# Block-causal attention with a Fourier feed-forward on one core: the row maxima of two heads taken together, one exponential per piece, and PSUM banks in one pool

## The chip, the cores and the metric

The kernel runs on one core of one Trainium2 chip. The metric is the device time in microseconds; the time before is the median of three runs. The profile is that of one further execution. The five engines are named as in the profile: PE is TensorE (matmuls, with PEld for its weight loads), DVE is VectorE, ACT is ScalarE, POOL is GpSimd, SP is SyncE, which here issues most DMAs. PSUM, which PE writes, has eight banks of 128 partitions x 512 float32.

## The reference

```python
def _attn_ref(q, k, v):            # (8 batches, 8 heads, 576 positions, 64)
    scores = scale * q @ k^T       # scale = 1 / 8
    mask = block_i >= block_j      # blocks of 64 positions
    scores = np.where(mask, scores, -1e9)
    scores = scores - np.max(scores, axis=-1, keepdims=True)
    attn = np.exp(scores); attn = attn / (np.sum(attn, -1, keepdims=True) + 1e-09)
    return attn @ v

x = heads side by side             # (8, 576, 512)
X = np.fft.fft(np.fft.fft(x, axis=1), axis=2)
u = x + np.real(X)
un = (u - mean) / np.sqrt(var + 1e-6)          # over the last axis
out = u + np.maximum(un @ w_ch1, 0.0) @ w_ch2  # 512 -> 2048 -> 512
```

## The kernel before

Most of it is near-float32 precision made of smaller parts: in attention and feed-forward a value is split into a high and a low float16 part ("ph" and "pl" for the probabilities, "uh" and "ul", "gh" and "gl", "VH" and "VL"), and a product is three matmuls.

**Attention.** 64 heads go one after another, in pairs (g = h // 2) where they share a load. `load_pair` brings q and k of two heads to 128 partitions, 64 for each head. `sum_qk` and `scale` find a power of two, `high` and `low` write the two float16 parts into two pair tiles, `a` (high q, then low k) and `b` (low q, then high k). `high_copies` and `low_copies` are DMAs that lay each head out again for the matmuls, as a "lead" tile (64 rows of high parts, then 8 rows of masks and one row for the maxima) and a "rest" tile. From them `max_part` computes a head's scores of the high parts alone, in four parts of one PSUM bank each. Queries are taken in five tiles j of 128 rows that start 64 before a multiple of 128, so the block at the end of a tile's keys is allowed only for its upper 64 rows; the mask rows in "lead" add a large negative number there, which makes the matmul 72 rows deep. DVE reduces each bank to row maxima, "M". `shift` turns M by a small matmul ("ident, M", 5 columns), ACT scales it to "mt", and a DMA writes mt into the last row of "lead". Then `scores` makes the real scores in four pieces of up to 512 columns (two matmuls per chunk, rest and lead), ACT takes the exponential twice, once to float16 (ph) and once to float32 (p), and POOL makes pl = p - ph. `values` multiplies by V (the "av" matmuls) and divides by the sums.

**Fourier.** After the eight heads of a batch, `mirror` reads the rows back, `folded` adds and subtracts mirrored halves (cosine and sine folds, tiles "fs"), `stage1` and `stage2` are matmuls with tables of cosines and sines ("dft"), and the result is added to x in "u". Cosine folds and sine folds share the tiles fs0 and fs1, so for batches 1 to 7 the order is cosine folds, cosine stage 1, sine folds, sine stage 1.

**Feed-forward.** `normalized_steps` normalizes 256 rows and transposes them; they are a "feed", numbered me = 1 to 18. A feed's first half writes "h" tiles (two 128-column groups of hidden units in one bank), ACT and DVE take them out as gh and gl; the second half accumulates in "acc". The last three feeds use a form with seven products in place of eight.

**The order.** The build keeps a clock of its own and queues with assumed costs for each engine. Work is cut into steps; a `Step` has an emit function, PE cost, a chain of costs on other engines ("D0.65" is 0.65 us on DVE, "B" marks where its bank is free again), the steps it comes after, whether it needs a PSUM bank, and a place. Ten lanes (loads, pairs, copies, maxima, scores, values, transforms) each hold one next step. The loop takes the step with the lowest place among those that are ready by the assumed clock, and otherwise a step of the feed ("filler"). The order found is then fixed on every engine. The banks: 3 "ps" for attention and Fourier, 2 "h" and 2 "acc" for feeds, 1 "av"; until the first feed starts, attention may use all seven of the first three kinds (`lent`).

The parts of a head's maxima before (tile j, first key, last key):

```python
MAXPARTS = (((0, 0, 64), (4, 512, 576), (1, 0, 192)), ((2, 0, 320),), ((3, 0, 448),), ((4, 0, 512),))
```

Line 229 is the helper that issues every matmul, line 232 that of the transposes, line 203 the wrapper of every other engine's instruction, so the profile's groups are told apart by their tiles.

Of the kernel before, what the change touches and what calls it, by code (L numbers as in the profile page):

```python
# [51 lines left out]

SEVEN = range(15, 18)

# [97 lines left out]
class Step:  # L152
# [8 lines left out]
    bank: bool = False  # L161
# [48 lines left out]
def tile_attn_fourier_ffn(  # L210
# [7 lines left out]
    ps = {name: pool(name, n, space=PSUM) for name, n in BANKS.items() if name != "ps"}  # L218
    turned = [(pool(f"ps{i}", 1, space=PSUM), f"ps{i}") for i in range(BANKS["ps"])]
    dram = pool("dram", 3, space=DRAM)  # L220

    def ps_tile():
        if current == "ps":
            turned.append(turned.pop(0))
            return turned[-1][0].tile([P, 512], F32, name=turned[-1][1])
        return ps[current].tile([P, 512], F32, name=current)
# [39 lines left out]
    def half_tiles(i):  # L266

        if i not in halved:
            a = work.tile([P, (64 + 2 * S) // (1 if i < HF else 2)], F32, name=f"lead{i}", bufs=1).bitcast(F16)
            b = work.tile([P, 2 * S // (1 if i < HF else 2)], F32, name=f"rest{i}", bufs=1).bitcast(F16)  # L270
            halved[i] = (a[0:KS, 0:64 + 2 * S], b[:, 0:2 * S]) + ((a[:, 64 + 2 * S:64 + 4 * S], b[:, 2 * S:]) if i < HF else ())
# [6 lines left out]
    def split(g):  # L278

        if g == GF:  # L280
            return tuple(stage[i].rearrange("p c d -> p (c d)").bitcast(F16)[:, 0:2 * S] for i in range(2))
        return half_tiles(g % 2)[2:4]

    M = [const.tile([P, 6], F32R, name=f"M_{i}") for i in range(2)]
# [3 lines left out]
    ZT = const.tile([P, NCOS], F32R, name="ZT")  # L288
    for i in range(HF):
# [18 lines left out]
    current = "ps"  # L308
    rings = {name: [0.0] * n for name, n in BANKS.items()}
# [8 lines left out]
    def ready(step):  # L318
        r = max((done[x] for x in step.after), default=0.0)
        if step.bank:  # L320
            return max(r, min(rings[x][0] for x in lent))
# [27 lines left out]
    def issue(step):  # L349
        nonlocal current, now  # L350
# [7 lines left out]
        free = None  # L358
        starts = []
        for engine, cost in step.chain:  # L360
            if engine == "B":
                free = t + HOP
# [15 lines left out]
        if step.bank:  # L378
            current = min(lent, key=lambda x: rings[x][0])
            rings[current] = rings[current][1:] + [t if free is None else free]  # L380
# [48 lines left out]
    def high(g):  # L429
        (rq, rk), sc = raws["pair", g], scales[g]  # L430
        a, b = split(g)
        scalar.activation(a[:, 0:S], rq, AF.Copy, scale=sc[:, 1:2])
# [4 lines left out]
    def low(g):  # L437
        (rq, rk), sc = raws.pop(("pair", g)), scales[g]
        a, b = split(g)
        vector.scalar_tensor_tensor(b[:, 0:S], rq, sc[:, 1:2], a[:, 0:S], op0=ALU.mult, op1=ALU.subtract)  # L440
        yield
        vector.scalar_tensor_tensor(a[:, S:], rk, sc[:, 2:3], b[:, S:], op0=ALU.mult, op1=ALU.subtract)
        yield

    def high_copies(h):
# [5 lines left out]
        sync.dma_start(x[0:D, 64:64 + S], a[at, 0:S])  # L451
# [3 lines left out]
    def low_copies(h):  # L455
# [3 lines left out]
        sync.dma_start(x[D:P], a[at])  # L459
# [161 lines left out]
    def max_part(h, n):  # L621

        m = M[h % 2]
# [25 lines left out]

    def shift(h):  # L650

        t = ps_tile()
        mm(t[0:5, 0:P], M[h % 2][:, 0:5], ident_r, start=True, stop=True)
# [26 lines left out]
    def scores(h, n):  # L680
# [78 lines left out]
    def score_lane():  # L759
        for h in range(B * H):  # L760
            for n, (i, at, chunks) in enumerate(PIECES):
                w = sum(x[2] for x in chunks)
                yield Step(
                    lambda n=n: scores(h, n), w / 1200.0, (_a(w), "p1", _a(w), "B", _g(w), "p"),
# [4 lines left out]
    def max_lane():  # L769
        for h in range(B * H):  # L770
# [5 lines left out]
            yield Step(lambda: shift(h), 0.12, ("A0.26", "B", "Q0.6", "M0.05", "L1.6"), (("M", h),), ("X", h), True, place=h - 0.6)  # L776

# [13 lines left out]
    def fourier_steps(b):  # L791
# [23 lines left out]
        def folded(op, width, name, c):  # L815
# [128 lines left out]
        def folds(name, op, width):  # L944
            for c in (2, 0, 1):
                yield Step(
                    lambda c=c: folded(op, width, name, c), 0.0, ("t1",) + (("X1.6", "A1.2", "X0.9") if c == 2 else ("X1.12", "A0.41", "X0.43")) + ("t",), (D_("u"),) + ((("F", 1),) if b == 1 else ()),
# [631 lines left out]
```

## Time and profile before

| | us |
|---|---|
| median of 3 runs | 1211.73 (1210.74 to 1212.89) |
| the profiled execution | 1207.94 |
| its span, first to last instruction | 1206.1 |
| PE busy | 1138.9 (94%) |
| DVE busy | 742.1 (62%) |
| ACT busy | 604.5 (50%) |
| POOL busy | 482.5 (40%) |
| mean granted PE clock | 0.961 of full |

The page cuts the span into 40 slices of about 30 us and gives each engine's busy share in tenths. Matmuls overlap in PE's pipeline, so a matmul's duration is longer than what it keeps the next one waiting. A row of the timeline has the start, the duration, the engine, the line, what is written from what, rows x columns of the weights, the shape that streams, and the number of instructions merged into it; in square brackets, idle time before it and what ended it.

### The profile page before, as it was taken

The numbers are of one execution on the slowest core, as the hardware profiler recorded it, in microseconds if no ns is written. First come the engines' busy times: TensorE is split into PE (matmuls) and PEld (weight loads), VectorE is DVE, ScalarE is ACT, GpSimd is POOL, SyncE is SP. The second block draws the span as 40 slices with busy tenths as digits, with TensorE's granted clock in tenths as the row PEclk, the third lists the DMA queues.
The fourth block names the chain that finished last, engine by engine and source line by source line (L and its number), as shares of the span: only waits on it lengthen the run. The fifth ranks groups of instructions, "written<-read, shape, count | busy, mean of one in ns | idle before, by whom it ended". The sixth has DMA issues, their size and how long they took to land.

```text
span 1206.1 us, 26181 instructions
## 1 busy us (share of the span) xinstructions
PE 1138.9 (94%) x10338; PEld 840.6 (70%) x10338; DVE 742.1 (62%) x1615; ACT 604.5 (50%) x1338; POOL 482.5 (40%) x630
## 2 busy tenths in 40 slices
PE   5767788999899999999999999999999999999998
PEld 4544475676677777777777777777677767788885
DVE  6877886666847673666647475757475657454421
ACT  5656667755565555536555346545554323233320
POOL 4552624534434434243442424353334333545420
PEclk9758789999799999999999999999999999999999
DMA  8785453333323342323325133413240010000000
GB/s 260 224 246 170 144 132 99 95 111 89 109 57 118 95 115 67 86 66 104 90 67 158 34 85 112 128 31 104 69 124 16 29 40 19 23 10 10 18 18 18
DMA packets 66128, 108.27 MB, mean 90 GB/s; under 512 B 9671, under 2 KB 36209, under 8 KB 66006
## 3 DMA queue, kind: packets, MB, share of 16 engines
q1 hardware_dynamic: 58662, 82.25, 24.1%
q10 hardware_dynamic: 4384, 16.78, 4.2%
q0 software_dynamic: 2960, 7.58, 2.1%
q8 instruction: 81, 1.33, 0.5%
q14 instruction: 41, 0.34, 0.1%
HBM read 58.50 MB, written 18.89 MB: 64 GB/s over the span
## 4 chain that ended last, share of the span: by engine, by line
PE 83%; DVE 5%; DMA 4%; POOL 3%; ACT 3%; issue 1%; SPq 0%; ACTq 0%; DVEq 0%; POOLq 0%
PE h L229 30%; PE acc L229 28%; PE ps L229 16%; PE av L229 8%; DMA lead<-mt 2%; DVE W L203 1%; POOL u L203 1%; PE ps L232 1%; DVE M L203 1%; POOL pl L203 1%; ACT p L203 1%; ACT ph L203 1%; ACT W L203 1%; DVE VL L203 1%; DMA lead<-rest 1%
## 5 line engine op out<-in xcount | busy, mean ns | idle before, releaser
L229 PE MATMUL h<-uh,W 128*128 128x256 f16 x2304 | 432.2, 274 | 0.2 <-DVE gl L203 0.2
L203 POOL TENSOR_TENSOR pl<-p,ph 128x288 f16<-128x288 f32 (+1 forms) x256 | 259.4, 1024 | 365.3 <-ACT p L203 337.0
L229 PEld LDWEIGHTS <-W 128*128 128x128 f16 x3456 | 332.7, 98 | 60.4 <-issue 1.3
L229 PE MATMUL h<-ul,W 128*128 128x256 f16 x1152 | 315.3, 274 | 0.0
L229 PE MATMUL acc<-W,gh 128*128 128x512 f16 (+1 forms) x1008 | 289.5, 370 | 0.0
L203 DVE TENSOR_REDUCE M<-ps 128x1 fp32r<-128x320 f32 (+3 forms) x293 | 131.3, 484 | 119.3 <-PE ps L229 118.8
L229 PE MATMUL acc<-W,gl 128*128 128x512 f16 (+1 forms) x504 | 186.2, 370 | 0.0
L229 PE MATMUL ps<-lead 73*128 73x288 f16 (+8 forms) x708 | 161.4, 291 | 15.4 <-DMA lead<-in_c_masks_dram 6.8
L203 ACT ACTIVATE ph<-ps 128x288 f16<-128x288 f32 (+1 forms) x235 | 119.5, 510 | 111.4 <-PE ps L229 110.6
L203 ACT ACTIVATE gh<-h 128x512 f16<-128x512 f32 x138 | 82.5, 598 | 166.6 <-PE h L229 161.6
L203 DVE SCALAR_TENSOR_TENSOR gl<-h,gh 128x512 f16<-128x512 f32 x138 | 94.7, 687 | 114.9 <-ACT gh L203 114.3
L229 PEld LDWEIGHTS <-ph 128*128 128x128 f16 x2112 | 133.1, 103 | 26.8 <-issue 4.6
L229 PEld LDWEIGHTS <-gh 128*128 128x128 f16 x1056 | 98.4, 99 | 67.8 <-issue 4.7
L229 PE MATMUL av<-VH,pl 128*128 128x65 f16 (+1 forms) x963 | 117.0, 201 | 8.4 <-POOL pl L203 6.5
L203 ACT ACTIVATE p<-ps 128x288 f32<-128x288 f32 (+1 forms) x235 | 119.0, 508 | 2.2 <-POOL pl L203 1.0
L229 PE MATMUL av<-VH,ph 128*128 128x65 f16 (+1 forms) x966 | 118.4, 203 | 0.7 <-ACT p L203 0.7
L229 PE MATMUL av<-VL,ph 128*128 128x64 f16 x960 | 116.7, 200 | 0.0
L229 PEld LDWEIGHTS <-pl 128*128 128x128 f16 x1056 | 103.5, 102 | 12.7 <-POOL pl L203 8.5
L229 PE MATMUL ps<-rest 128*128 128x320 f16 (+3 forms) x356 | 99.4, 292 | 1.0 <-DVE M L203 0.9
L229 PEld LDWEIGHTS <-lead 73*128 73x128 f16 (+1 forms) x744 | 66.7, 103 | 36.4 <-issue 8.1
L229 PEld LDWEIGHTS <-gl 128*128 128x128 f16 x528 | 51.5, 98 | 55.3 <-issue 0.5
L229 PEld LDWEIGHTS <-rest 128*128 128x128 f16 x372 | 38.8, 104 | 34.9 <-issue 15.3
(255 smaller groups left out, 1611.1 us busy)
## 6 DMA issues: line engine op xcount, KB each, us to landing
raw<-in_qk_dram SPq DMA_DIRECT2D x30, 576.0 KB
W<-in_moe_w_ch_dram ACTq DMA_DIRECT2D x14, 1024.0 KB
V<-in_v_dram SPq DMA_DIRECT2D x32, 320.0 KB
rest<-lead SPq DMA_DIRECT2D x64, 144.0 KB
rest<-rest SPq DMA_DIRECT2D x60, 144.0 KB
out_dram<-u SPq DMA_DIRECT2D x32, 256.0 KB
xd<-x SPq DMA_DIRECT2D x30, 256.0 KB
lead<-lead SPq DMA_DIRECT2D x60, 72.0 KB
```

The lines of the kernel that those rows point to most:

```text
L203: x = f(*args, **kw)
L229: return tc.keep_in_program_order(nc.tensor.matmul(*args, **kw))
L232: return tc.keep_in_program_order(nc.tensor.transpose(*args, **kw))
```

## The change

- `pair_max` replaces `max_part` for pairs g >= 8, which are heads 16 to 63. It reads the pair tiles a and b directly, 64 rows for each head: head 0 of the pair on rows 0 to 63, head 1 on rows 64 to 127, each into a bank of its own, their matmuls issued in turn. The mask rows are gone: the five blocks that only the upper 64 rows may see are matmuls of their own and are reduced for partitions 64 to 127 alone (DIAG); the rest goes to MAIN, and M is the larger of both. A head then has 9 matmuls in place of 6, with the same 1600 columns.
- To serve as weights with queries from 64 before the start, tile a gets 64 zero columns ahead (`high`, `low`, `sum_qk` and the copies move by 64; a memset on POOL for the first three pairs).
- M has four buffers in place of two.
- From head 17 on, `scores` takes one exponential, to float32, and a copy on ACT makes the float16 part from it; the bank is free after the exponential.
- After feed 2 the "h" banks join "ps" in one pool of five. From then on an "h" tile takes the bank that is free first and holds it until gh and gl are made. A pair's maxima need two banks of one pool at once; while such a step has its inputs, steps that need one bank and have a higher place stand back.
- All batches now order the Fourier work as cosine folds, sine folds, cosine stage 1, sine stage 1; the sine folds of batches 1 to 7 take tiles from "un" (those of the normalized rows), and come after the transposes of the feed before.
- The first steps of `weight_parts` take their bank one yield earlier.

```diff
+ONCE = 17
+LEAST = -3.0e38
+GP = 8
...
-    M = [const.tile([P, 6], F32R, name=f"M_{i}") for i in range(2)]
+    M = [const.tile([P, 6], F32R, name=f"M_{i}") for i in range(4)]
+    MAIN, DIAG = ([const.tile([P, 5], F32, name=f"{x}_{i}") for i in range(2)] for x in ("MAIN", "DIAG"))
...
+    for i in range(2):
+        gpsimd.memset(MAIN[i], LEAST)
+        gpsimd.memset(MAIN[i][0:64, 0:1], 0.0)
+        gpsimd.memset(DIAG[i], LEAST)
     for i in range(HF):
         gpsimd.dma_start(LEAD[i][D:KS], c_masks)
...
     def sum_qk(g):
         (rq, rk), acc = raws["pair", g], sums(g)
         a, b = split(g)
-        scalar.activation(a[:, 0:S], rq, AF.Square, accum_out=acc[:, 1:2])
+        if g < GF + 3:
+            gpsimd.memset(a[:, 0:64], 0.0)
+        scalar.activation(a[:, 64:64 + S], rq, AF.Square, accum_out=acc[:, 1:2])
...
+    PAIRPARTS = (((0, 0, 64), (1, 128, 192), (2, 256, 320), (3, 384, 448), (4, 512, 576), (1, 0, 128)), ((2, 0, 256),), ((3, 0, 384),), ((4, 0, 512),))
+
+    def pair_max(g, n):
+
+        a, b = split(g)
+        ts = [ps_tile() for _ in range(2)]
+        at = 0
+        for i, (j, lo, hi) in enumerate(PAIRPARTS[n]):
+            for x, t in enumerate(ts):
+                rows_ = slice(D * x, D * (x + 1))
+                mm(
+                    t[:, at:at + hi - lo], a[rows_, P * j:P * (j + 1)], b[rows_, S + lo:S + hi], start=(i == 0),
+                    stop=(i == len(PAIRPARTS[n]) - 1), skip_group_check=True,
+                )
+            at += hi - lo
+        yield
+        for x, t in enumerate(ts):
+            main, diag = MAIN[x], DIAG[x]
+            if n == 0:
+                vector.tensor_reduce(
+                    diag[64:128], t[64:128, 0:320].rearrange("p (x y) -> p x y", y=64), axis=AX.X, op=ALU.max
+                )
+                vector.tensor_reduce(main[:, 1:2], t[:, 320:448], axis=AX.X, op=ALU.max)
+            else:
+                vector.tensor_reduce(main[:, n + 1:n + 2], t[:, 0:P * (n + 1)], axis=AX.X, op=ALU.max)
+            if n == 3:
+                vector.tensor_tensor(M[(2 * g + x) % 4][:, 0:5], main, diag, op=ALU.max)
+            yield
...
-        scalar.activation(ph[:, at:at + w], t[:, 0:w], AF.Exp, scale=0.125)
-        yield
+        if h < ONCE:
+            scalar.activation(ph[:, at:at + w], t[:, 0:w], AF.Exp, scale=0.125)
+            yield
         p32 = work.tile([P, 512], F32, name="p32", bufs=2)
         scalar.activation(p32[:, 0:w], t[:, 0:w], AF.Exp, scale=0.125)
         yield
+        if h >= ONCE:
+            scalar.copy(ph[:, at:at + w], p32[:, 0:w])
+            yield
         gpsimd.tensor_tensor(pl[:, at:at + w], p32[:, 0:w], ph[:, at:at + w], op=ALU.subtract)
...
+        for g in range(GP, B * H // 2):
+            for n in range(4):
+                d = f"D{(0.78, 0.42, 0.56, 0.91)[n]}"
+                yield Step(
+                    lambda n=n: pair_max(g, n), 0.06 + sum(x[2] - x[1] for x in PAIRPARTS[n]) / 2400.0, (d, "B", d),
+                    (("hi", g),), ("M", 2 * g) if n == 3 else None, 2, place=2 * g - 1.6,
+                )
...
-                if b == 0 and name == "s":
-                    t = work.tile([P, 2, 256], F32R, name="uh", bufs=2)
+                if name == "s":
+                    t = work.tile([P, 2, 256], F32R, name="un" if b else "uh", bufs=2)
...
-        order = (folds(*cos), folds(*sin), stages("c"), stages("s")) if b == 0 else (folds(*cos), stages("c"), folds(*sin), stages("s"))
+        order = (folds(*cos), folds(*sin), stages("c"), stages("s"))
...
-                gs[f] = ps["h"].tile([P, 512], F32, name="h")
+                gs[f] = ps_tile() if me > 2 else own_tile()
...
+        if not shared_out and ("F", 2) in done:
+            shared_out.append(True)
+            rings["ps"] += rings.pop("h")
...
+        claim = min((heads[i].place for i in able if heads[i].bank == 2 and max(done[x] for x in heads[i].after) <= now), default=None)
+        if claim is not None:
+            able = [i for i in able if heads[i].bank != 1 or heads[i].place <= claim]
```

More of the change, by code (lines that the diff above doesn't have):

```diff
@@ L160 @@
     key: object = None
-    bank: bool = False
+    bank: int = 0
+    hold: object = None
+    drop: object = None
     need: tuple = ()
@@ L217, in tile_attn_fourier_ffn, with next_banks, first @@
     ps_av = pool("ps_av", 1, space=PSUM)
-    ps = {name: pool(name, n, space=PSUM) for name, n in BANKS.items() if name != "ps"}
-    turned = [(pool(f"ps{i}", 1, space=PSUM), f"ps{i}") for i in range(BANKS["ps"])]
+    accs = pool("acc", BANKS["acc"], space=PSUM)
+    rings = {name: [[0.0, pool(f"{name}{i}", 1, space=PSUM), f"{name}{i}"] for i in range(BANKS[name])] for name in ("ps", "h")}
+    rings["acc"] = [[0.0, accs, "acc"] for _ in range(BANKS["acc"])]
+    given, held, shared_out = [], {}, []
     dram = pool("dram", 3, space=DRAM)
     def ps_tile():
[L223 to L226, printed above, removed]
+        _, pool_, name = given.pop(0)
+        return pool_.tile([P, 512], F32, name=name)
+    def next_banks(n):
+        def first(x):
+            return (sorted(rings[x], key=lambda y: y[0]) if shared_out else rings[x])[:n]
+        return min(((x, first(x)) for x in lent if len(rings[x]) >= n), key=lambda x: max(y[0] for y in x[1]))
     def mm(*args, **kw):
@@ L320, in ready @@
         if step.bank:
-            return max(r, min(rings[x][0] for x in lent))
+            return max(r, *(x[0] for x in next_banks(step.bank)[1]))
         if step.place > H and not step.cost:
@@ L357, in issue @@
                 x.forget(now)
-        free = None
+        free = []
         starts = []
@@ L378, in issue @@
         if step.bank:
-            current = min(lent, key=lambda x: rings[x][0])
-            rings[current] = rings[current][1:] + [t if free is None else free]
+            ring, got = next_banks(step.bank)
+            rings[ring] = [x for x in rings[ring] if not any(x is y for y in got)] + got
+            for n, x in enumerate(got):
+                x[0] = float("inf") if step.hold else free[min(n, len(free) - 1)] if free else t
+            if step.hold:
+                held[step.hold] = got[0]
+            given[:] = got
+        if step.drop in held:
+            held.pop(step.drop)[0] = t
         parts = step.emit()
@@ L769, in max_lane @@
     def max_lane():
-        for h in range(B * H):
+        for h in range(2 * GP):
             for n in range(4):
@@ L1073, in second @@
             if f == 0:
-                acc.append(ps["acc"].tile([P, DM], F32, name="acc"))
+                acc.append(accs.tile([P, DM], F32, name="acc"))
             gh, gl = gs[f]
@@ L1191, in both_steps @@
                     after = (("t", me, 0), ("t", me, 1)) + ((("g", me, k - 2),) if k > 1 else ())
-                yield Step(lambda part=part: both(k, part), 0.654, (), after, ("h", me, k) if last else None)
+                yield Step(
+                    lambda part=part: both(k, part), 0.654, (), after, ("h", me, k) if last else None, 0 if part else 1,
+                    hold=None if part else ("h", me, k),
+                )
         def split_steps(k):
@@ L1211, in feed_steps @@
             if not seventh:
-                seventh.append(turned.pop(0))
-                taken.append(rings["ps"].pop(0))
+                one = min(rings["ps"], key=lambda x: x[0])
+                rings["ps"] = [x for x in rings["ps"] if x is not one]
+                seventh.append(one[1:])
             nk = NF // 2
@@ L1525, in tile_attn_fourier_ffn @@
             if len(lent) > 1:
-                now = max(now, ready(filler), *rings["h"], *rings["acc"])
+                now = max(now, ready(filler), *(x[0] for x in rings["h"] + rings["acc"]))
                 lent = ["ps"]
```

49 lines of the change are left out of this document (28 added, 21 removed).

## The prediction

> **What bounds the kernel now.** I read the page's busy shares first, then its slices.
>
> ```profile
> PE 1138.9 (94%) x10338; PEld 840.6 (70%) x10338; DVE 742.1 (62%) x1615; ACT 604.5 (50%) x1338; POOL 482.5 (40%) x630
> PE   5767788999899999999999999999999999999998
> PEclk9758789999799999999999999999999999999999
> PE 83%; DVE 5%; DMA 4%; POOL 3%; ACT 3%; issue 1%; SPq 0%; ACTq 0%; DVEq 0%; POOLq 0%
> ```
>
> TensorE (PE) is the only engine near full and carries 83% of the chain that ended last. But the slices show three stages: up to about 240 us PE has holes and a low granted clock, one more dent follows near 300 us, and then it is solid. The table by stretches gives the sizes (columns: length, busy us and count of each engine, granted clock, DMA share, GB/s).
>
> ```profile
> core 0: us, PE busy (x) PEld busy (x) DVE busy (x) ACT busy (x) POOL busy (x), PEclk, DMA share, GB/s
> 240.00:290.00 50.00, 50.00 (x480) 36.26 (x478) 31.64 (x78) 26.65 (x63) 16.19 (x18) 1.00 0.28 81
> 290.00:304.00 14.00, 10.42 (x109) 7.82 (x107) 10.98 (x26) 8.10 (x20) 10.08 (x14) 1.00 0.59 167
> 304.00:318.00 14.00, 10.60 (x80) 7.29 (x80) 12.37 (x29) 7.83 (x20) 7.73 (x12) 0.52 0.54 151
> 330.00:1040.00 710.00, 710.00 (x6665) 517.40 (x6663) 431.78 (x976) 344.94 (x786) 273.17 (x330) 1.00 0.28 78
> ...
> L203 ACT ACTIVATE mt<-ps x48: 249/266/267, 242.0 to 934.8; 5x128 f16<-5x128 f32 x48
> ```
>
> From 330 to 1040 us PE is busy 710.00 of 710.00 at full clock: every us of PE work taken out there ends the kernel one us sooner, and time saved on any other engine is worth nothing. The last row (one "mt" is made per head, after its maxima) puts the 48 heads of the third to eighth batch at 242 to 935 us, so nearly all of the changed maxima lie in this stage; only one pair of heads falls into the dent at 290 to 318 us. There PE loses 14 - 10.42 = 3.6 us, then 14 - 10.60 x 0.52 = 8.5 us of full-clock time.
>
> **The maxima on PE.** A pipelined matmul's duration says little; its cost is the distance to the next start (timeline of PE, steady state; columns start, duration, ..., count of merged ones).
>
> ```profile
> 510.62 0.30 PE L229 MATMUL ps<-lead 72*128 72x64 f16 x3
> 510.76 0.60 PE L229 MATMUL acc<-W,gh 128*128 128x512 f16 x2
> 511.20 0.38 PE L229 MATMUL acc<-W,gl 128*128 128x512 f16 x1
> 511.41 0.59 PE L229 MATMUL acc<-W,gh 128*128 128x512 f16 x2
> ...
> 512.71 0.30 PE L229 MATMUL ps<-lead 72*128 72x320 f16 x1
> 512.85 0.27 PE L229 MATMUL h<-uh,W 128*128 128x256 f16 x1
> 512.96 0.27 PE L229 MATMUL h<-ul,W 128*128 128x256 f16 x1
> ...
> 514.97 0.57 PE L229 MATMUL ps<-lead 72*128 72x448 f16 x2
> 515.38 0.20 PE L229 MATMUL av<-VH,ph 128*128 128x65 f16 x1
> 515.41 0.19 PE L229 MATMUL av<-VL,ph 128*128 128x64 f16 x1
> ```
>
> One head's six matmuls (64, 64 and 192 columns; 320; 448 and 512) take 0.14 + 0.14 + 0.41 = 0.69 us for 1600 columns, so a pair of heads costs 1.38 us. The change streams the same 1600 columns per head in nine matmuls (five of 64, then 128, 256, 384, 512), the two heads on different halves of PE's rows. The trace has no matmul on half the rows, so its price is bounded. If the halves overlap fully, a pair costs one head's 0.69 and saves 0.69; if not at all, five at 0.03 (the "av" rows' distance, each with its own weights), 0.06, 0.11 (the 256-column row), 0.16 (interpolated) and 0.22 (three of 512 in 0.65) give 0.70 a head and no saving. I take a point between: 64-column couples can't overlap, since no distance below about 0.03 us shows, and in each longer couple the second starts one such step late. That is 10 x 0.03 + (0.06 + 0.11 + 0.16 + 0.22) + 4 x 0.03 = 0.97, a saving of 0.41 per pair and, for the 23 pairs in the solid stages, -9.4 us; the ends are 0 and -15.9.
>
> Going from whole rows to halves and back happens in four places per pair, 8 x 23 = 184 times. The nearest row is the 5-column matmul of "shift" among whole-array ones:
>
> ```profile
> 538.56 0.23 PE L229 MATMUL ps<-ident,M 128*5 128x128 f32 x1
> 538.63 0.20 PE L229 MATMUL av<-VH,ph 128*128 128x65 f16 x1
> 538.67 0.20 PE L229 MATMUL av<-VL,ph 128*128 128x64 f16 x1
> ```
>
> It takes 0.07 us and the next 0.04 where 0.03 is usual, so some 0.01 per passage: +1.8 us. The upper end is a full emptying of the pipeline, 0.16 us (the three maxima at 510.62 end at 510.92, and their follower had started at 510.76): +29.4 us. Zero is the lower end. I take the measured neighbour. Against it speaks the Trainium skill, TensorEngine Tiling (Array Packing), section Tiling Modes: a change of tiling mode drains TensorE. No run here shows it; by that rule the sum would get the upper end, and it is the slower rival below. For the overlap itself, the Trainium skill, TensorE: Matmul & The Clock Gate, Part 3, says matmuls on different row groups start about 4 ns apart, which no row here shows; by that figure the maxima would save close to the -15.9.
>
> **DVE, ACT, POOL: nothing.** Groups by form:
>
> ```profile
> L203 DVE TENSOR_REDUCE M<-ps 128x1 fp32r<-128x512 f32 x58 | 39.7, 685 | 21.3 <-PE ps L229 21.2
> L203 DVE TENSOR_REDUCE M<-ps 128x1 fp32r<-128x448 f32 x59 | 36.4, 617 | 10.2 <-PE ps L229 10.2
> L203 DVE TENSOR_REDUCE M<-ps 128x1 fp32r<-128x320 f32 x58 | 28.2, 486 | 19.5 <-PE ps L229 19.3
> L203 DVE TENSOR_REDUCE M<-ps 128x1 fp32r<-128x192 f32 x59 | 20.5, 347 | 0.0
> L203 DVE TENSOR_REDUCE M<-ps 128x2 fp32r<-128x128 f32 x59 | 17.0, 288 | 68.4 <-PE ps L229 68.2
> L203 ACT ACTIVATE ph<-ps 128x512 f16<-128x512 f32 x121 | 72.8, 603 | 27.5 <-PE ps L229 26.8
> L203 ACT CAST ph<-x 128x512 f16<-128x512 f32 x24 | 14.8, 618 | 37.5 <-POOL x L203 37.5
> ```
>
> Before, a head's five reductions take 2.42 us; after (320, 128, about 0.42 for 256 and 0.55 for 384 by interpolation, 512) 2.43, and the closing maximum stays one small instruction. One exponential per piece replaces an exponential by a copy: 618 for 603 ns, 188 pieces, +3 us at most on an ACT that is busy 345 of 710 us while PE is not waiting for it; uncovered it would cost those 3. "ph" comes one instruction (0.6 us) later, but "pl", which PE needs as well, is the third of three instructions both times. The bank is free that 0.6 us earlier, which only matters if PE waits for banks. The maxima no longer wait for the copies to "lead", only for "hi"; the shift's DMA still does, so SP's queue has the same transfers in nearly the same order. The three added POOL memsets before 80 us lie on an engine busy 40%. Four buffers for "M" and the tile that weight_parts takes a step earlier move no instruction.
>
> **Shared banks.** PE had no idle between 330 and 1040 us, so nothing can be gained; lost can be that feed-forward's "h" tiles, which had two banks of their own, now find all five taken by maxima, two at a time. Some 120 "h" tiles (12 feeds x 8, 3 x 8); lower end 0, upper end one 0.6 us evacuation each, 72 us, far away since a bank is held only about 1.5 us at a time. I take +1.
>
> **The earlier sine folds.** Here batch 1 counts, whose feed fills the dent.
>
> ```profile
> 264.88 1.19 DVE L203 TENSOR_TENSOR fs<-tmp,fs 128x257 fp32r<-128x257 f32 x1 [1.86 <-ACT fs L203]
> ...
> 271.65 0.68 DVE L203 TENSOR_TENSOR tmp<-X,U 33x512 f32<-33x512 f32 x1
> ...
> 282.03 0.42 DVE L203 TENSOR_TENSOR fs<-tmp,fs 128x256 fp32r<-128x256 f32 x1
> ...
> 302.85 0.22 PE L229 MATMUL ps<-ident,M 128*5 128x128 f32 x1 [2.29 <-DVE M L203]
> ...
> 317.85 0.27 PE L229 MATMUL h<-uh,W 128*128 128x256 f16 x1
> ```
>
> The sine folds start at 271.65, after the cosine stage has freed "fs", though the cosine folds end at 264.88 + 1.19 = 266.07: 5.6 us of wait. With tiles of their own they follow at once, and feed 3, which starts at 317.85, comes 5.6 us sooner if the rest of the chain keeps its length. At the loss rate of 304 to 318 us, 8.5 / 14 = 0.61, that is -3.4 us; ends 0 (the chain is late elsewhere, the cosine evacuations that are now behind the folds on DVE for one) and -12.1, the whole dent. Later batches transform beside a full PE: 0.
>
> **Start.** Six memsets go ahead of the mask DMAs on POOL, for which PE waits first.
>
> ```profile
> 0.31 0.10 POOL L1561 MEMSET const-bfloat16-1.0<- 128x1 bf16 x1
> 0.34 0.10 POOL L1561 MEMSET const-uint8-127<- 128x1 uint8 x1
> ...
> PE ps L229 <- DMA lead<-in_c_masks_dram: 6.8, 1, 6.8
> ```
>
> At 0.03 apart to 0.10 each, 0.2 to 0.6 us: +0.3.
>
> **Sum:** -9.4 + 1.8 + 1.0 - 3.4 + 0.3 = -9.7 us, so the profiled execution would go from 1207.94 to 1198.2, and the median, which stands 3.8 us above it, from 1211.73 to 1202.0.
>
> **Rivals.** Changes within 0.2% (2.4 us) count as the same, about what this measurement can tell.
> - Passages empty PE (slower): in place of +1.8 the passages cost 184 x 0.16 = 29.4, so 1211.73 - 9.4 + 29.4 + 1.0 - 3.4 + 0.3 = 1229.6; it decides from (9.4 + 3.4 - 1.3) / 184 = 0.06 us per passage, where the sum is zero. For it: matmuls overlap their tails by 0.16 us now, and that is what would be lost. Against: the 5-column matmul passes at 0.01.
> - Halves don't overlap, so the change doesn't do what it says: 1211.73 + 1.8 + 1.0 - 3.4 + 0.3 = 1211.4, the same. For it: no overlapping matmuls in the trace. Against: different rows, different banks, no operand shared.
> - Full overlap, and the dent mostly gone (half clock never granted: -8.5): 1211.73 - 15.9 - 8.5 + 0.3 = 1187.6. For it: the clock fell only after the 2.3 us idle before 302.85, which a sooner feed could shorten. Against: small matmuls' distance of 0.03.
>
> **How the numbers follow.** Forecast 0.50 (1196 to 1207), full overlap 0.15, emptying 0.22 (at part or all of its price, 1213 to 1230), no overlap 0.13 (same 0.10, slower 0.03 if passages cost a little as well). Faster 0.65, same 0.10, slower 0.25. The range 1188 to 1221 leaves out the lower half of the full overlap (0.08) and the dearer half of the emptying (0.11).
>
> **What would show it.** In the changed profile: starts of the two halves' matmuls 0.03 us or less apart, and the four parts of a pair taking about 0.97 us together; a start after such a part 0.01 and not 0.16 late; PE still busy all of its time from 330 us on (a wait of "h" for ACT or DVE would mean banks); sine folds ending near 276 us and the first "h" of feed 3 near 312 us. The prediction is wrong if the half-row matmuls follow each other at their full lengths or behind a gap, or if the dent stays or moves.

## The result, and the profile after

| | before | after |
|---|---|---|
| median of 5 runs each, same chip | 1210.74 us (1207.33 to 1212.89) | 1222.92 us (1219.79 to 1224.42) |
| ratio | | 1.0103, 95% interval 1.0083 to 1.0123 |
| profiled execution | 1207.94 us | 1224.42 us |

The change makes the kernel 12 us slower, 21 us above the forecast of 1202.0 and 1.9 us outside its range. The busy shares and slices of the changed kernel's page:

```profile
span 1222.6 us, 26637 instructions
PE 1140.5 (93%) x10482; PEld 826.4 (68%) x10482; DVE 752.3 (62%) x1615; ACT 624.3 (51%) x1338; POOL 486.4 (40%) x639
PE   5667788999799999999999999999999999999998
PEclk9758899999799999999999999999999999999999
PE 79%; DVE 9%; DMA 4%; POOL 3%; ACT 2%; issue 2%; SPq 1%; ACTq 0%; DVEq 0%; POOLq 0%
```

PE is still the only engine near full. Its busy time rose by 1.6 us only (1138.9 to 1140.5) while the span grew by 16.5 (1206.1 to 1222.6): 14.9 us of the 16.5 are time in which PE stands idle. 7.8 of them lie before 240 us, where the changed kernel falls behind by 3.5 us of work only, so further down I count work as well as idle time. On the chain DVE has gone from 5% to 9%. The same stretches as before, from the table by stretches:

```profile
core 0: us, PE busy (x) PEld busy (x) DVE busy (x) ACT busy (x) POOL busy (x), PEclk, DMA share, GB/s
290.00:304.00 14.00, 11.73 (x127) 8.60 (x125) 12.90 (x30) 7.40 (x18) 7.33 (x10) 1.00 0.67 183
304.00:318.00 14.00, 9.30 (x104) 5.75 (x102) 6.69 (x16) 9.08 (x18) 10.68 (x14) 0.76 0.12 33
318.00:330.00 12.00, 7.99 (x102) 5.87 (x101) 11.72 (x24) 7.27 (x17) 8.70 (x13) 0.78 0.17 48
330.00:1040.00 710.00, 705.12 (x6706) 501.19 (x6705) 440.12 (x978) 363.01 (x787) 273.47 (x326) 1.00 0.29 80
```

The row of before that goes with the third one:

```profile
318.00:330.00 12.00, 12.00 (x125) 9.52 (x123) 8.93 (x20) 6.14 (x13) 5.41 (x8) 1.00 0.20 47
```

The solid stage from 330 us has a leak of 710 - 705.12 = 4.9 us, where before had none. The dent was to shrink; it is wider. From 290 to 318 us it loses a little less than before, 14 - 11.73 = 2.3 and 14 - 9.30 x 0.76 = 6.9 us of full-clock time, but it goes on to 330 us and loses 12 - 7.99 x 0.78 = 5.8 more. What feeds it, on DVE and PE ("ps<-uh,W" is an "h" tile on a bank of the common pool):

```profile
265.05 0.67 DVE L211 TENSOR_TENSOR tmp<-X,U 33x512 f32<-33x512 f32 x1
277.04 0.68 DVE L211 TENSOR_TENSOR tmp<-X,U 33x512 f32<-33x512 f32 x1
327.79 0.27 PE L244 MATMUL ps<-uh,W 128*128 128x256 f16 x1
```

The sine folds (second row) do come straight behind the cosine folds (first), but those are late by themselves (before they started at 254.66): batch 1's sine folds start at 277.04 instead of 271.65, and feed 3's first h matmul at 327.79 instead of 317.85. I counted the PE work other than maxima that is left at a time (each matmul as its columns at 53.5 ns per 128, the rate found below, plus 2.5 ns; that fits the usual distances of 109 ns after 256 columns and 216 after 512). The changed kernel is behind by 3.5 us at 240 us, by 10.6 at 345 and by 18.5 at 1040, when both have done all maxima; it gets 2.0 back in the tail. So 10.6 us were lost by the end of the dent and 7.9 between 345 and 1040 us, 4.9 of these idle. That idle time is not the pairs' alone: experiment 1 below, which has no pairs and takes the time of before, idles 695 - 690.62 = 4.4 us in the same stretch, where before idles nothing.

```profile
345.00:1040.00 695.00, 690.62 (x6426) 502.34 (x6423) 427.77 (x950) 343.58 (x748) 272.49 (x331) 1.00 0.27 77
```

Against experiment 1 the change is 12.6 us of work behind at 345 us and loses only 3.6 more by 1040 us.

**What the half-row matmuls cost.** Timeline of PE in the changed kernel (start, duration, ..., merged count; 64*128 marks half rows, and the pair tiles a and b have the names "lead" and "rest" here):

```profile
500.46 0.19 PE L244 MATMUL av<-VL,ph 128*128 128x64 f16 x1
500.49 0.19 PE L244 MATMUL av<-VH,pl 128*128 128x65 f16 x1
500.62 0.34 PE L244 MATMUL ps<-rest,lead 64*128 64x384 f16 x2
500.88 0.20 PE L244 MATMUL av<-VH,ph 128*128 128x65 f16 x1
...
501.70 0.19 PE L244 MATMUL av<-VL,ph 128*128 128x64 f16 x1
501.73 0.20 PE L244 MATMUL av<-VH,pl 128*128 128x65 f16 x1
501.86 0.39 PE L244 MATMUL h<-rest,lead 64*128 64x512 f16 x1
501.86 0.39 PE L244 MATMUL ps<-rest,lead 64*128 64x512 f16 x1
```

The two halves of a part start in the same hundredth of a microsecond (501.86 and 501.86; 3 to 4 ns apart in the records). And both borders show: after an "av" of 65 columns the next start usually comes 0.03 us later, but 0.13 later where the next is half-row (500.49 to 500.62, 501.73 to 501.86). The medians over all undisturbed stretches from half-row start to next whole-row start are 215 ns for two of 256 columns, 269 for two of 384 and 322 for two of 512. That is 53.5 ns more per 128 columns, one head's streaming, so the overlap is complete; and it leaves 215 - 107 = 108 ns that do not depend on the columns, the border out. The border in takes 96 ns (128 instead of 32). With part 0 (12 matmuls, 308 ns) a pair's maxima cost 308 + 215 + 269 + 322 + 4 x 96 = 1.50 us, where two single heads cost 1.38. (The trace shows 87 stretches for the 96 parts, since a few parts follow another directly; nine stretches less at 0.20 make 1.8 us less in all.) **Halves that overlap fully still lose, because each stretch pays 0.20 us for two borders and saves one head's columns once:** 0.19, 0.11, 0.16 and 0.21 us in the four parts (448, 256, 384 and 512 columns).

### The profile page after: what moved, and what is told of

Read it like the earlier page. It is cut to its first block, busy times and chain, and to the rows that moved or that the text cites. A ratio compares the mean times of both kernels' runs of the same rounds, so it can differ in the third digit from the quotient of the medians.

```text
span 1222.6 us, 26637 instructions
## 1 busy us (share of the span) xinstructions
PE 1140.5 (93%) x10482; PEld 826.4 (68%) x10482; DVE 752.3 (62%) x1615; ACT 624.3 (51%) x1338; POOL 486.4 (40%) x639
## 4 chain that ended last, share of the span: by engine, by line
PE 79%; DVE 9%; DMA 4%; POOL 3%; ACT 2%; issue 2%; SPq 1%; ACTq 0%; DVEq 0%; POOLq 0%
PE acc L244 27%; PE ps L244 26%; PE h L244 18%; PE av L244 7%; DVE W L211 2%; DMA lead<-mt 1%; DVE M L211 1%; POOL u L211 1%; POOL pl L211 1%; DVE MAIN L211 1%; DMA lead<-rest 1%; DMA u<-in_moe_w_ch_dram 1%; DVE VL L211 1%; DVE lead L211 1%; PE ps L247 1%
## 5 line engine op out<-in xcount | busy, mean ns | idle before, releaser
L244 PE MATMUL ps<-uh,W 128*128 128x256 f16 x1216 | 223.7, 274 | 0.5 <-DVE ul L211 0.5
L244 PE MATMUL h<-uh,W 128*128 128x256 f16 x1088 | 201.5, 275 | 1.5 <-ACT bs L211 1.3
L244 PE MATMUL ps<-ul,W 128*128 128x256 f16 x608 | 166.6, 274 | 1.4 <-DVE ul L211 1.3
L244 PE MATMUL h<-ul,W 128*128 128x256 f16 x544 | 149.4, 275 | 0.0
L211 DVE SCALAR_TENSOR_TENSOR gl<-ps,gh 128x512 f16<-128x512 f32 x76 | 52.2, 687 | 90.6 <-ACT gh L211 90.4
L211 ACT ACTIVATE gh<-ps 128x512 f16<-128x512 f32 x76 | 45.1, 594 | 116.9 <-PE ps L244 116.8
L211 ACT CAST ph<-p 128x512 f16<-128x512 f32 (+1 forms) x188 | 98.3, 523 | 5.2
L244 PEld LDWEIGHTS <-lead 64*128 64x128 f16 (+2 forms) x888 | 56.7, 100 | 54.3 <-issue 26.3
L244 PE MATMUL ps<-lead 73*128 73x320 f16 (+12 forms) x309 | 78.1, 304 | 14.3 <-DMA lead<-in_c_masks_dram 7.1
L211 DVE SCALAR_TENSOR_TENSOR gl<-h,gh 128x512 f16<-128x512 f32 x62 | 42.6, 688 | 73.5 <-ACT gh L211 73.5
```

Of the source, the lines that this page charges most:

```text
L211: x = f(*args, **kw)
L244: return tc.keep_in_program_order(nc.tensor.matmul(*args, **kw))
```

## The experiments

Each time is a median beside the kernel before on the same chip; the ratio is to that one. Diffs are against the changed kernel, unless another is named.

**1. No pairs.** `-GP = 8` / `+GP = 32`: all other parts of the change stay.

> All maxima by max_part as before, the rest of the change kept (GP = 32). Theory P (the pairs themselves cost: each passage between whole and half rows holds PE 0.1 us, so a pair takes 1.50 us and not 1.38, and pair 8's maxima, placed ahead of head 15, delay batch 1's transform by some 8 us): the 2.7 us of PE time, most of the 6.4 us that the dent near 300 us grew by, and the waits of PE after 330 us go, 1205 to 1211 us. Theory B (the shared banks cost: feeds and attention wait for each other's banks): 1216 to 1221 us, with PE waits after 330 us still there. Theory S (the earlier sine folds crowd DVE and ACT in front of attention): 1216 to 1221 us as well, with the dent as it is in the changed kernel.

1209.84 us (10 runs), ratio 0.9996 (0.9978 to 1.0014): the kernel before. Everything lost comes through the pairs, and the rest of the change together is worth nothing measurable. It is not idle-free, though: by my count of work it is 2.0 us ahead of before at 345 us, loses 4.3 of work by 1040 us and gets 2.7 back in the tail.

**2. Own banks for h.** `gs[...] = own_tile()` for all feeds, `shared_out` never set: "h" keeps two banks, attention has three.

> The changed kernel with two banks of their own for h all through, three for the rest; pairs, one exponential and sine folds kept. Theory P: 1220 to 1226 us, since nothing on which it rests is touched, and two of three banks at a time for a pair may cost a little more. Theory B: the 4.9 us of PE waits after 330 us go, 1214 to 1219 us. Theory S: no change, 1221 to 1225 us.

1259.84 us, ratio 1.0414 (1.0377 to 1.0451): 37 us slower than the change. The pairs need the shared pool badly: with three banks their last maxima come at 1004 us and not at 875. The time is then lost behind that, since PE idles 30.1 us after 1040 us (4.1 in the change) but no more than the change between 345 and 1040 us (4.7 and 4.9). **Without pairs** (own banks and GP = 32):

> No pairs and no shared banks: the kernel before with the earlier sine folds and one exponential alone. The earlier sine folds won some 5 us in old_folds against the change; if they do so here, 1203 to 1207 us. If the dent is set by other things than the folds: 1208 to 1212 us, as before. Shared banks without pairs left 4.5 us of PE waits after 330 us (no_pairs); with own banks these should be under 1 us.

1211.46 us, ratio 1.0025 (1.0008 to 1.0043). Without pairs, sharing costs nothing that these runs can tell; the difference to experiment 1 is 1.6 us the other way. PE's idle time from 345 to 1040 us did not go below 1 us, as I had expected: it is 4.6 us, all of it one wait for gl. Feed 3 starts at 312.61 us, and the work left at 345 us is 3.4 us less than before:

```profile
312.61 0.42 PE L244 MATMUL h<-uh,W 128*128 128x256 f16 x1
```

**3. Two exponentials.** `-ONCE = 17` / `+ONCE = 64`: the bank of a score piece is held 0.6 us longer, as before.

> The changed kernel with two exponentials per piece for all heads, none replaced by a copy (ONCE = 64). Theories P, B and S: within 0.2% of the changed kernel, 1220 to 1226 us, as the copy takes 0.02 us more than the exponential on an ACT that is half idle. If the bank that the exponential frees 0.6 us earlier is what keeps the shared banks going: 1227 us or more, with more PE waits after 330 us. If the later ph holds PE's values back: 1217 us or less.

1230.84 us, ratio 1.0181 (1.014 to 1.0221), 8 us slower than the change. I had put this edit at nothing; with pairs waiting for two banks at once, 0.6 us of a bank per piece is dear: PE idles 9.8 us from 345 to 1040 us instead of 4.9. No run changes this alone without pairs.

**4. Old order of the folds** for batches 1 to 7 (`order = (folds(*cos), stages("c"), folds(*sin), stages("s"))`, tiles shared again):

> The changed kernel with the order of before for batches 1 to 7: cosine folds, cosine stage 1, sine folds, sine stage 1, on shared fs tiles. Theory P: the sine folds' earlier place won some 6 us in batch 1's chain, so without it feed 3 starts later than 327.8 us and the time is 1224 to 1230 us. Theory S: 1214 to 1219 us. Theory B: 1221 to 1225 us.

1227.49 us, ratio 1.0149 (1.013 to 1.0169). The new order is worth 4.6 us within the change, near my 3.4, but not by what I had in mind: feed 3 starts no later with the old order (327.39 us, in the change 327.79), and the work left at 345 us is the same within 0.3 us.

```profile
327.39 0.27 PE L244 MATMUL ps<-uh,W 128*128 128x256 f16 x1
```

The difference comes later, as idle time of PE between 345 and 1040 us: 9.0 us instead of 4.9.

**5. Only late pairs**, `GP = 12`: the 20 pairs that lie behind most of the dent.

> The changed kernel with pairs from the fourth batch on (GP = 12, heads 24 to 63, 20 pairs instead of 24), so that no pair lies before or in the dent near 300 us. Theory D (most of the 12 us were lost in the dent: pair 8's maxima go ahead of heads 14 and 15, so batch 1's transform and feed 3 start 10 us later): feed 3 starts near 317 us as without pairs (316.5), and the time is 1209.8 + 20 x 0.12 for the passages + 1 to 3 for waits = 1212 to 1216 us. Theory E (the loss is spread evenly over the pairs, 0.5 us each): 1209.8 + 20 x 0.55 = 1219 to 1223 us.

1218.05 us, ratio 1.0069 (1.0052 to 1.0085), feed 3 from 318.4 us, and the work left at 345 us is that of before within 0.3 us: the dent is as before, and 8 us are lost all the same. The passages explain at most 20 x 0.12 = 2.4. PE idles 8.3 us from 345 to 1040 us, where experiment 1 idles 4.4; that is 3.9 more, and some 2 us stay unexplained.

**6. Heads one after the other**, against experiment 5: the loop over the two heads goes outside the loop over the matmuls. Only part 0 has more than one matmul per head.

```diff
-        for i, (j, lo, hi) in enumerate(PAIRPARTS[n]):
-            for x, t in enumerate(ts):
+        for x, t in enumerate(ts):
+            at = 0
+            for i, (j, lo, hi) in enumerate(PAIRPARTS[n]):
```

> As pairs_late, but within each part all matmuls of the pair's first head are issued before those of the second, so the two halves of the rows cannot run side by side except at the one border. If the halves overlap fully when they alternate: 0.5 to 0.69 us more per pair, 10 to 14 us above pairs_late. If they gain nothing from alternating (the rival, that the half-row matmuls are limited by issue or weight loads): the same as pairs_late within 3 us.

1217.17 us, ratio 1.0056 (1.0039 to 1.0073): no difference to experiment 5. The timeline of PE says why it couldn't tell the theories apart ("h" is the bank of the first head here, "ps" that of the second):

```profile
410.91 0.26 PE L244 MATMUL h<-rest,lead 64*128 64x64 f16 x3
410.99 0.20 PE L244 MATMUL ps<-rest,lead 64*128 64x64 f16 x1
411.01 0.19 PE L244 MATMUL h<-rest,lead 64*128 64x64 f16 x1
411.03 0.19 PE L244 MATMUL ps<-rest,lead 64*128 64x64 f16 x1
411.04 0.19 PE L244 MATMUL h<-rest,lead 64*128 64x64 f16 x1
411.06 0.19 PE L244 MATMUL ps<-rest,lead 64*128 64x64 f16 x1
411.07 0.22 PE L244 MATMUL h<-rest,lead 64*128 64x128 f16 x1
411.09 0.28 PE L244 MATMUL ps<-rest,lead 64*128 64x64 f16 x3
```

The program has six of "h" and then six of "ps"; PE starts the second head's while the first head's still run. The stretch takes 381 ns at the median instead of 308, less than the 509 that heads in series would take (308 and once more the 201 ns that one head's six matmuls take of it, an estimate from the distances above). Over 20 pairs 73 ns each are 1.5 us, too little for this comparison.

**7. Half as many passages**, against experiment 5: two steps per pair of two parts and four banks each. The edit also raises the PE cost that the planner assumes, from 0.06 to 0.2 us per step beside the columns, and lets the rule of standing back apply to steps of four banks.

```diff
-        ts = [ps_tile() for _ in range(2)]
+        both_ = [(n, [ps_tile() for _ in range(2)]) for n in (2 * m, 2 * m + 1)]
+        for n, ts in both_:
...
-                    lambda n=n: pair_max(g, n), 0.06 + sum(x[2] - x[1] for x in PAIRPARTS[n]) / 2400.0, (d, "B", d),
-                    (("hi", g),), ("M", 2 * g) if n == 3 else None, 2, place=2 * g - 1.6,
+                    lambda m=m: pair_max(g, m), 0.2 + sum(x[2] - x[1] for n in (2 * m, 2 * m + 1) for x in PAIRPARTS[n]) / 2400.0,
+                    (d, "B", d, "B", e, "B", e, "B"), (("hi", g),), ("M", 2 * g) if m else None, 4, place=2 * g - 1.6,
```

> As pairs_late, but a pair's four parts are issued as two steps of two parts with four banks, so PE passes between whole and half rows four times per pair and not eight. Theory of the passages (0.1 us each, 0.2 us per stretch): 20 x 0.4 = 8 us less on PE than pairs_late, 1204 to 1209 us, if the four banks cost nothing. If four of five banks at a time keep feeds and scores waiting: as pairs_late or slower, 1212 to 1225 us, with waits of PE for DVE's maxima.

1210.50 us (10 runs), ratio 1.0003 (0.9989 to 1.0016), 7.6 us faster than experiment 5 and the best kernel with pairs. Timeline of PE in it:

```profile
517.82 0.38 PE L244 MATMUL ps<-uh,W 128*128 128x256 f16 x2
518.04 0.27 PE L244 MATMUL ps<-ul,W 128*128 128x256 f16 x1
518.15 0.27 PE L244 MATMUL ps<-uh,W 128*128 128x256 f16 x1
518.35 0.38 PE L244 MATMUL ps<-rest,lead 64*128 64x64 f16 x12
518.56 0.27 PE L244 MATMUL h<-rest,lead 64*128 64x256 f16 x2
518.77 0.28 PE L244 MATMUL ps<-uh,W 128*128 128x256 f16 x1
```

A 256-column matmul keeps the next waiting 0.11 us (518.04 to 518.15), but 0.20 ahead of the half rows (518.15 to 518.35); the two of 256 columns inside the stretch follow the twelve at once, and the border out makes 0.21 of their 0.11 (518.56 to 518.77). One border pair less: 417 and 485 ns for the two stretches, with 2 x 96 ns 1.09 us per pair, 0.29 less than two single heads. PE idles 7.5 us from 345 us on, though, 3.3 of it on one wait, so nothing of the gain against before is left. **The same 1.0 earlier in place:**

> As merged, with the place of a pair's maxima one head earlier (2 g - 2.6), because attention ended later there (last batch's heads at 910 us where pairs_late has 842) and PE then waited 3.9 us at 1040 us for the last normalization. If that wait is an accident of the order: it goes, and the time is 1203 to 1208 us. If four banks at a time cost in another place as soon as the maxima come earlier: 1210 us or more.

1214.84 us, ratio 1.0057 (1.0035 to 1.008): dearer, not cheaper.

**8. What makes the pairs wait?** Against experiment 5, both free marks in the chain, `(d, "B", d, "B")`: the planner takes the second bank as free only after its own reduction.

> As pairs_late, but the planner counts a pair's two banks free one after the other, each after its own reduction; in the change both count as free after the first reduction, so the next tile can be put on a bank that DVE still reads. If that is what PE waits for (waits for MAIN after 330 us are 4.7 us in pairs_late): these waits go below 1.5 us and the time is 1213 to 1216 us. If the waits come from having too few banks: the same as pairs_late, 1217 to 1220 us, with the idle time under another name.

1219.18 us, ratio 1.0083 (1.0066 to 1.01): the same. The waits on DVE's MAIN vanish from the list of waits, and 6.0 us on another DVE step stand there instead. **The rule "one bank stands back"** (`-if claim is not None:` / `+if False:`), in the change, in experiment 5 and in experiment 7:

> The full change, but steps that need one bank no longer stand back when a pair of maxima is ready and waits for two. Theory A (standing back is what costs time beside the passages): 1214 to 1218 us. Theory B (it costs nothing, the banks and the pairs' own order do): 1221 to 1225 us. Its order differs from that of the changed kernel only from feed 3 on, so the dent near 300 us, with feed 3's first h matmul near 328 us, must stay in both; if it goes, the dent differs from run to run.

> Pairs from the thirteenth on (20 pairs), and no step stands back for a pair. With the rule this took 1218.05 us, 8.2 above no pairs, of which the passages give 20 x 0.12 = 2.4. Theory A (standing back makes the rest): 1212 to 1214 us. Theory B (it does not): 1217 to 1219 us.

> Pairs from the thirteenth on in two steps of four banks each (half as many passages), and no step stands back for them. With the rule this took 1210.50 us, the same as before. Theory A (standing back for four banks is what eats the gain of the fewer passages): 1205 to 1208 us, below the kernel before. Theory B (the wait for four free banks eats it in any case, and without the rule the pair waits longer still): 1210 to 1216 us.

1245.59 us, ratio 1.0309 (1.0267 to 1.0351); 1227.14, 1.0128 (1.0098 to 1.0158); 1219.34, 1.0075 (1.0051 to 1.01). All three are 9 to 23 us slower with it gone: theory A falls, and theory B, by which the rule does nothing, as well: the rule helps. (In the third, theory B had the direction right, not the size.) In the change I had expected the dent to stay, since the order would differ only from feed 3 on. That was wrong: the rule also holds for the early pairs, the orders part at 230 us, and feed 3 starts at 336.3 us instead of 327.8. PE's waits from 330 us on, first in the change, then in the same without the rule:

```profile
PE ps L244 <- DVE MAIN L211: 1.9, 3, 1.4
PE h L244 <- DVE MAIN L211: 0.2, 1, 0.2
```

```profile
PE ps L244 <- DVE MAIN L211: 8.7, 7, 2.7
PE h L244 <- DVE MAIN L211: 5.5, 5, 1.8
```

The wait on MAIN, for the reductions of a pair to give their banks back, goes from 2.1 to 14.2 us. It is a wait for banks. PE's idle time from 345 to 1040 us goes from 4.9 to 16.3 us with it, from 8.3 to 12.8 in experiment 5 and from 3.6 to 12.4 in experiment 7. The one edit that made the wait on MAIN vanish, the free marks above, left the time as it was.

**9. Why does the dent grow?** Three tries while it was open: the pairs 1.0 later in place, the banks joined a feed earlier (`("F", 1) in done`), and only the four pairs of the third batch (8 to 11) with single heads after them.

> The changed kernel (pairs from head 16 on) with the place of a pair's maxima at 2 g - 0.6 instead of 2 g - 1.6, that of single maxima, so pair 8's no longer come before head 15's scores. Theory D: feed 3 starts at 316 to 320 us and the time is 1213 to 1217 us. Theory E: 1220 to 1225 us.

> The changed kernel (pairs from head 16 on), but the h and ps banks join after feed 1 and not after feed 2, so that the first pairs, at 240 to 290 us, take two of five banks and no longer two of three. Theory: the dent grows in the change because those pairs leave batch 1's transform one bank of three; then feed 3 starts before 322 us (327.8 in the change, 318.4 in pairs_late) and the time is 1213 to 1218 us. Rival: the maxima's work and place themselves delay the transform, whatever the banks: feed 3 at 325 us or later, 1220 to 1226 us.

> Only the four pairs of the third batch (8 to 11) keep their common maxima; all heads after them take theirs one by one, as without the change. Theory (the four early pairs delay batch 1's chain and so make the dent near 300 us deeper, whatever comes after): what no pairs cost, 1209.8 us, plus the 4.9 us by which all pairs stand above twenty late ones: about 1214.7 us, and feed 3's first h matmul near 327 us. Rival (the dent grows only because later pairs pull work ahead of it, or it is an accident of the order): 1209 to 1212 us and feed 3 at 313 to 318 us.

1227.1 us, ratio 1.0139 (1.0122 to 1.0156); 1227.53, 1.0143 (1.0126 to 1.016): neither edit brings the time back (feed 3 starts at 325.4 us in the first). The four early pairs alone take 1223.28 us, ratio 1.01 (1.0074 to 1.0126): **as much as all 24**, and their dent is that of the change. The stretch from 240 to 345 us, in the changed kernel and then with the early pairs alone, has PE busy 94.01 and 94.00 of 105 us:

```profile
240.00:345.00 105.00, 94.01 (x912) 66.17 (x910) 67.92 (x156) 60.45 (x135) 47.11 (x58) 0.92 0.33 93
```

```profile
240.00:345.00 105.00, 94.00 (x899) 66.00 (x899) 66.11 (x152) 59.58 (x132) 46.69 (x58) 0.92 0.34 95
```

(The order of DVE's instructions is the same in both up to 342 us.) So, against experiment 1, 13 us for the first four and 8 for the last twenty make 13 for all, not 21: they do not add up. With the early pairs alone PE idles 5.0 us from 345 to 1040 us, with all 24 it idles 4.9.

**10. The first pair.** In the change heads 16 and 17 go on PE before the scores of head 15, the last of batch 1. PE in the changed kernel, then in the kernel before:

```profile
230.24 0.38 PE L244 MATMUL ps<-rest,lead 64*128 64x64 f16 x12
...
238.99 0.37 PE L244 MATMUL ps<-rest,lead 64*128 64x512 f16 x1 [1.39 <-DVE MAIN L211]
...
239.95 0.29 PE L244 MATMUL ps<-rest 128*128 128x288 f16 x1
240.07 0.29 PE L244 MATMUL ps<-lead 73*128 73x288 f16 x1
```

```profile
231.24 0.29 PE L229 MATMUL ps<-rest 128*128 128x288 f16 x1
231.37 0.29 PE L229 MATMUL ps<-lead 73*128 73x288 f16 x1
```

Head 15's scores begin at 239.95, not 231.24, behind the pair's last part, which itself waits 1.39 us for a bank. Its sums then come at 249.1 us instead of 240.8 (rows of tile "DEN", after and before):

```profile
L211 DVE TENSOR_SCALAR DEN<-av,vacc x1: 225/225/225, 249.1 to 249.1; 128x5 f32<-128x5 f32 x1
```

```profile
L203 DVE TENSOR_SCALAR DEN<-av,vacc x1: 226/226/226, 240.8 to 240.8; 128x5 f32<-128x5 f32 x1
```

From there to feed 3 it is 78.7 us after and 77.1 before; so 8.3 of the 9.9 us by which feed 3 is late are head 15's. Two runs test whether that is the cause: the first pair held back until head 15's last scores are issued (`(("hi", g),) + ((("S", 15, 2),) if g == GP else ())`), and heads 16 and 17 single (`GP = 9`).

> The full change, but the first pair (heads 16 and 17) may only start once head 15's last scores are issued; all other pairs as in the change. Theory (the first pair, whose place is before head 15, holds two banks' worth of the queue and pushes the last head of batch 1 back by 8 us, and batch 1's chain with it): head 15's output at 240 to 243 us, feed 3's first h matmul at 318 to 322 us, and 1215 to 1219 us, the time of the change without the early pairs. Rival (each of the early pairs delays the chain, whatever its order against head 15): head 15's output at 240 to 243 us as well, but feed 3 at 324 to 329 us and 1220 to 1225 us.

> Pairs from the ninth on: heads 16 and 17 take their maxima one by one, all later heads in pairs (23). Theory (only the first pair's place before head 15 hurts): head 15's output at 238 to 242 us, feed 3 at 316 to 320 us, 1214 to 1218 us. Rival (the pairs of heads 18 to 23 delay the chain by themselves): feed 3 at 322 to 328 us, 1219 to 1224 us.

1243.79 us, ratio 1.027 (1.0235 to 1.0304); 1231.02, 1.018 (1.015 to 1.0209): **the theory falls as a way to the time.** With 23 pairs, head 15's sums come at 241.1 and feed 3 starts at 316.17 us, as forecast, and yet the kernel is 8 us slower than the change: PE waits 6.2 us for MAIN within the dent and idles 12.5 us after 345 us. With the first pair held back head 15 is at 244.1 us, but feed 3 only at 348.1, later than either theory had it. The delay moves, it does not go.

**What stays open.** The cost beside the borders depends on the order that the planner finds, and each edit of that order gave another time. The nine variants in which pairs start with the third batch and h shares its banks (the change, 3, 4, the first of the three without the rule, the three of 9, and 10) lie between 1222.9 and 1245.6 us, none near 1210. That pairs want two banks at once from a pool of five, and that this can cost waits, is shown (experiments 3 and 8); that such waits make the 12 us of the change itself is not, as it idles hardly more in the solid stage than the kernel without pairs. That the first pair makes feed 3 late is shown by the run without it (316.17 us); why the time is lost elsewhere then is not. One rival stands untested. The planner assumes 4 x 0.06 + 1600 / 2400 = 0.91 us of PE for a pair where the trace has 1.50, and 2 x (4 x 0.03 + 1600 / 2400) = 1.57 for two single heads where it has 1.38, so it counts 0.6 us too little for each pair and 0.2 too much for two single heads. In experiment 7 it assumes 1.07, near the 1.09 measured, and that is the one order with pairs that takes the time of before; its two variants with the same assumption took 1214.84 and 1219.34 us. No run changed this cost alone.

## Why the prediction was wrong

- **Overlap, -9.4 us (0.97 us for a pair's maxima): mis-sized, the gain is larger.** I let 64-column couples not overlap and longer ones start 0.03 us late. They start 3 to 4 ns apart, and one head's columns are all that is paid, the end that I had put at -15.9. The Trainium skill, TensorE: Matmul & The Clock Gate, Part 3, gives about 4 ns between row groups; the trace agrees, with its 3 to 4.
- **Passages, +1.8 us (0.01 us each): the step that failed.** I took the 5-column matmul of "shift" as the nearest row. But that one uses all 128 rows, so it never passed between whole and half rows. The measured price is 96 ns in and 108 ns out, ten times mine and above the 0.06 at which I had said the slower rival decides. Both terms together: at most 24 x (1.50 - 1.38) = +2.9 us, and 1.8 less for the parts that follow another directly, so some +1 to +3 instead of -7.6. The Trainium skill, TensorEngine Tiling (Array Packing), section Tiling Modes, says that a change of mode drains TensorE; the trace agrees in direction, with 0.1 us per border, and experiment 7 puts a time on it: 72 stretches become 40, which is 32 x 0.20 = 6.5 of its 7.6 us.
- **Shared banks, +1 us: the wrong question.** I costed what "h" loses to the pairs. A pair holds two banks through two reductions in a row, and waits for two; I put no term there. It shows when banks get scarcer or the rule goes (experiments 3 and 8), and with late pairs alone (3.9 us more idle time than without pairs). In the change itself the waits on MAIN after 330 us are only 2.1 us, and its 4.9 us of idle time are nearly those of the kernel without pairs.
- **One exponential, 0: wrong by 8 us within the change** (experiment 3). I wrote that a bank free earlier "only matters if PE waits for banks"; the pairs made it wait.
- **Earlier sine folds, -3.4 us: the second step that failed.** Without pairs and with own banks (experiment 2) the term comes out: feed 3 is at 312.6 us, where I had put it, and 3.4 us of work are won by 345 us. With shared banks and no pairs (experiment 1) it is 2.0 us, with feed 3 at 316.5. Within the change it buys no time in the dent, and that experiment 4 comes near it with 4.6 us is luck, as those lie behind the dent. I expected feed 3 at 312 us from an unchanged start of batch 1's chain, and wrote of the pairs only that "one pair of heads falls into the dent". I didn't ask what the pair of heads 16 and 17, moved ahead of head 15, pushes back on PE. That is a step that was moved, and what it was moved past was the last head of the batch whose chain fills the dent. Feed 3 came at 327.8, and at 345 us the kernel was 10.6 us behind where I had it 3.4 ahead. This and the first two terms are more than the 21 us by which the forecast was off; the tail gave 2.0 back.
- **Start, +0.3:** PE's first wait for the masks is 7.1 us instead of 6.8, as forecast.
- **The cover in the solid stage:** "nothing can be gained" on other engines was right, but a stage without idle time can still lose: 4.9 us, and 4.4 without pairs. What the rest of the change does there I had put at nothing.
- **The rivals:** the time is nearest the slower rival (1229.6), and its mechanism is part of the cause, at two thirds of its price. It alone explains little, since the overlap that went with it was full; most of the loss is the late chain in the dent (10.6 of the 18.5 us of work by which the kernel is behind at 1040 us), which no rival held.

## What to carry to other kernels

A change between whole and half rows costs 0.1 us each way, so two 64-row matmuls side by side pay only in stretches with well over 0.2 us of streaming saved; count stretches, not matmuls, and put parts together before splitting rows. Two things that need PSUM at once hold it through two evacuations, so price the banks as well as the PE time. And where the order is made by a planner, look first at what the moved step now stands ahead of: one pair before the last head of a batch delayed that batch's sums by 8 us, yet moving it back alone bought nothing. And give the planner the measured price of a new kind of step; here it counted a pair at 0.91 us that took 1.50, and what that cost was not tested.

## What the hardware showed that was not expected

- The border between whole and half rows: 96 ns in, 108 ns out, the same for stretches of 2 matmuls of 256, 384 and 512 columns.
- PE does not keep the program's order between the two halves of its rows: in experiment 6 the second head's matmuls start 77 ns after the stretch's start, before three of the first head's six, which stand ahead of them in the program (76 or 77 ns in all ten stretches where the banks tell the heads apart). The Trainium skill, TensorE: Matmul & The Clock Gate, Part 3, calls matmuls strictly ordered in start and end; the starts in this trace differ.
